# A retention layer and a rational feed-forward on one core: four head units kept whole, values scaled on VectorE, a one-step weight join, and a new order for steps 0 to 31

## The chip, the cores and the metric

One core of a Trainium2 chip runs the whole program. The metric is the device time of one execution in microseconds (us); the time of a kernel is the median of its runs. Engines are called PE (TensorE matmul), PEld (TensorE weight load), DVE (VectorE), ACT (ScalarE), POOL (GpSimd) and SP (SyncE, which issues every DMA here).

## What is computed

```python
scores = scale * q @ k^T                       # 8 batches x 8 heads, 576 positions, 64 wide
ret    = scores * gamma[h] ** (i - j)          # for i >= j, else 0
x      = (ret @ v), heads side by side         # 4608 tokens x 512
h = x @ w_in                                   # 512 -> 2048
P = a0 + a1 h + a2 h^2 + a3 h^3
Q = 1 + |b0| |h| + |b1| h^2
out = (P / (Q + 1e-6)) @ w_out                 # 2048 -> 512
```

All arrays are float32. Dense products are made from two parts of each operand, high and low (tile type fp32r): high by high, high by low and low by high, three matmuls of 128x512 for one.

## The kernel before, in words

**Units.** The 4608 tokens are 36 units of 128 tokens; a batch with its 8 heads is 4.5 units. Unit n has a tile `qk` (q and k transposed, by pairs of heads) and a tile `kv` (k and v with tokens on partitions), each 512 KB, loaded by `load_unit` (lines 104 to 113). The decay is split up: `scale_q` (182) multiplies q by gamma^i on POOL, `scale_v` (187) multiplies v by gamma^-j, eight ACTIVATE instructions of 128x64 with one head's factor each (lines 190 and 191), and what is left of the decay is a mask of zeros and ones. A running state S (64x64 for each head) carries what earlier units give; `fade` (362) multiplies it by gamma^128 on POOL.

**A unit's attention.** A unit is cut in two halves of 64 tokens, so that all its products are 64x64 and four of them can stand in the array. `visit(None, k)` (288) makes the scores of unit k (16 matmuls) and the state's addends (16, less in a batch's first and last half); `decay` (314) multiplies the scores by the mask, `middle` and `add` (331, 351) make the state at the half and at the end; `put` (304) makes the outputs: 24 to 32 matmuls. `emit` (261) interleaves the two rows of the array and sets a SyncE nop between matmuls of different rows that write one bank; SP's later DMAs stand behind these nops. `keep_hi` (342, ACT) and `keep_lo` (345, DVE) take the result out of PSUM as x's two parts.

**Weights.** Each of the 16 blocks of w_in and of w_out comes as 128 x 512 words of 64 bits (512 KB), loaded by `load_weight`. `split_weight` (144) makes two fp32r parts in four stages: ACT scales the high word into `c` with Abs and the low word into `low`; DVE joins them, `c<-c,bits` (line 158); DVE puts the sign back, `c<-bits,c` (line 160); ACT writes the high part `w`, and POOL the difference. The stages are called `split0` to `split3`; `start` begins new blocks.

**Steps.** A step is one block f (128 of the 2048 columns) of one group b of 512 tokens: `gemm1` (12 matmuls into a PSUM tile `h`), `ffn_p`, `ffn_p2`, `ffn_va`, `ffn_v`, `ffn_r`, `ffn_q`, `ffn_q3` for the rational function on ACT and DVE, `ffn_hi` and `ffn_lo` (two parts of `g`), and, three or four steps later, `gemm2` (12 matmuls into `acc`). There are 144 steps: 0 to 7 do half of group 0, 8 to 23 all of group 1, 24 to 31 the other half of group 0, and so on. PSUM tiles `h`, `y` (part of a visit) and the warm-up tile `unread` share two places: a gemm1 can begin when the one two before it has been read, the last reader of `h` being `ffn_p2` on DVE.

**The head.** Before step 0 the program does units 0 to 3 (`before(n)`, line 519, in the order `BEFORE`), with a few idle matmuls `unread` after each (`warm`), then the scores of unit 4 with the outputs of unit 3 (`LAST_BEFORE`). Steps 0, 2, 4 and 6 contain a visit each (outputs of units 4 to 7, scores of 5 to 7).

**What sets the order.** Every engine runs its instructions in program order (`InOrder`, line 59), and the order within a step is written out in lists of names: `FIRST` for steps 0 to 23 with a visit, `FIRST_ALONE` for those without, `MID` for steps 8 to 20, `DENSE` and `DENSE_ALONE` for steps 24 to 31, `REST` and `END` after that (lines 33 to 44; chosen at line 595).

Of the kernel before, what the change touches and what calls it, by code (L numbers as in the profile page):

```python
# [35 lines left out]
FIRST_ALONE = "split1 split3 gemm1 visit gemm2 ffn_p split2 ffn_va ffn_p2 ffn_hi decay keep_hi ffn_lo ffn_r scale_q decay1 add keep_lo fade start scale_v split0 ffn_q ffn_q3 ffn_v".split()
MID = "start split2 gemm1 ffn_p gemm2 ffn_r ffn_hi ffn_lo ffn_va split3 ffn_p2 ffn_q ffn_v ffn_q3 split0 split1".split()
DENSE = "gemm1 ffn_p visit decay split0 ffn_p2 split1 scale_q ffn_hi ffn_r ffn_va ffn_lo scale_v gemm2 ffn_q split2 ffn_v keep_hi split3 ffn_q3 keep_lo decay1 add fade".split()
DENSE_ALONE = "gemm1 ffn_p visit decay keep_hi decay1 add ffn_r split1 fade keep_lo split2 ffn_p2 split0 ffn_va ffn_v scale_q ffn_hi ffn_lo gemm2 split3 scale_v ffn_q ffn_q3".split()
# [598 lines left out]
```

## Time and profile before

| | us |
|---|---|
| median of 3 runs (lowest to highest) | 917.73 (916.36 to 919.26) |
| the profiled execution | 915.75 |
| its span | 913.9 |
| PE busy in the span | 888.9 (97%) |
| DVE busy | 801.1 (88%) |
| ACT busy | 696.2 (76%) |
| POOL busy | 154.3 (17%) |

The profile is one execution, 1.85 us longer than its span of instructions. A row of the timeline reads: start, duration, engine, line, operation, out<-in, count, and in brackets the idle time before it with what ended it. L67 is the line of the helper that records instructions, so work is told by its tiles. A matmul of 64x64 or 128x128 in float32 is two records; one of 128x512 in fp32r is one.

### The profile page before, as it was taken

The page shows a single profiled execution, that of the slowest core. Times are in us where ns is not written, and L with a number is a line of the kernel's source. Part 1 is how long each engine was busy: PE and PEld are TensorE (multiplying, and loading weights), DVE is VectorE, ACT ScalarE, POOL GpSimd, SP SyncE. Part 2 cuts the span into 40 slices and gives each one's busy share as a digit, 9 for nine tenths or more (in the row PEclk, how much of TensorE's full clock was granted, in tenths as well). Part 3 has the DMA queues.
Part 4 walks back from the last instruction along what each step waited for, and adds up shares of the span by engine and source line. Part 5 has one row for each costly group of instructions (what it writes and reads, how often), then busy time and mean ns, then how long its engine had stood idle before and what let it go on. Part 6 is the DMA issues. An engine that isn't in the chain of part 4 may idle for free.

```text
span 913.9 us, 19359 instructions
## 1 busy us (share of the span) xinstructions
PE 888.9 (97%) x7852; PEld 733.1 (80%) x7852; DVE 801.1 (88%) x1217; ACT 696.2 (76%) x1306; POOL 154.3 (17%) x128
## 2 busy tenths in 40 slices
PE   7888999999999999999999999999999999999997
PEld 6666778878888888888888888888888888888886
DVE  3699999998899988889888889889888998888895
ACT  5798899988667778777877787777877777667774
POOL 3556445551011110011100100010110111000000
PEclk8789999999999999999999999999999999999999
DMA  9985000014121112111211112011211121001001
GB/s 340 363 309 202 1 0 1 1 49 138 47 93 48 47 47 93 47 47 47 93 48 48 47 65 74 25 43 33 90 47 48 47 94 47 1 2 46 1 1 46
DMA packets 20569, 65.50 MB, mean 72 GB/s; under 512 B 2432, under 2 KB 2432, under 8 KB 20480
## 3 DMA queue, kind: packets, MB, share of 16 engines
q1 hardware_dynamic: 20480, 64.28, 20.0%
q8 instruction: 61, 1.00, 0.5%
q14 instruction: 28, 0.23, 0.1%
HBM read 54.83 MB, written 9.44 MB: 70 GB/s over the span
## 4 chain that ended last, share of the span: by engine, by line
PE 81%; DVE 13%; issue 2%; ACT 2%; DMA 1%; SPq 0%; ACTq 0%; DVEq 0%
PE acc L67 37%; PE h L67 35%; DVE p L67 6%; PE ps L67 4%; DVE v L67 3%; DVE c L67 3%; PE y L67 2%; PE psNone L67 2%; PE unread L67 1%; DMA gv_sb<-in_gv 1%; ACT free_at L67 1%; DMA bits<-in_w_out 0%; ACT v L67 0%; DVE qk L67 0%; ACT o L67 0%
## 5 line engine op out<-in xcount | busy, mean ns | idle before, releaser
L67 PE MATMUL acc<-w,g 128*128 128x512 f32 x1632 | 396.3, 392 | 0.5 <-DVE o L67 0.3
L67 PE MATMUL h<-xhi,w 128*128 128x512 f32 x1152 | 382.3, 393 | 10.4 <-DVE p L67 6.4
L67 PEld LDWEIGHTS acc<-w,g 128*128 128x128 f32 x1632 | 303.8, 188 | 65.6 <-issue 0.7
L67 PEld LDWEIGHTS h<-xhi,w 128*128 128x128 f32 x1152 | 218.4, 190 | 59.0 <-DVE p L67 8.0
L67 PE MATMUL h<-xlo,w 128*128 128x512 f32 x576 | 226.1, 393 | 0.0
L67 ACT ACTIVATE p<-h,ab_sb 128x512 f32<-128x512 f32 x144 | 111.9, 777 | 127.1 <-PE h L67 117.0
L67 DVE SCALAR_TENSOR_TENSOR p<-p,ab_sb,u 128x512 f32<-128x512 f32 x131 | 120.7, 922 | 15.0 <-ACT u L67 15.0
L67 PEld LDWEIGHTS h<-xlo,w 128*128 128x128 f32 x576 | 109.5, 190 | 22.8
L67 DVE TENSOR_TENSOR p<-p,h 128x512 f32<-128x512 f32 x144 | 98.9, 687 | 29.9 <-ACT u L67 28.9
L67 DVE TENSOR_TENSOR v<-v,u 128x512 f32<-128x512 f32 x131 | 94.7, 723 | 26.5 <-ACT v L67 26.5
L67 ACT ACTIVATE u<-h 128x512 f32<-128x512 f32 x131 | 77.9, 595 | 49.8 <-DVE v L67 49.1
L67 DVE SCALAR_TENSOR_TENSOR p<-p,ab_sb,h 128x512 f32<-128x512 f32 x144 | 107.6, 747 | 4.7
L67 ACT ACTIVATE v<-u,absb 128x512 f32<-128x512 f32 x131 | 105.8, 808 | 1.2 <-DVE p L67 1.1
L67 DVE SCALAR_TENSOR_TENSOR p<-v,p 128x512 f32<-128x512 f32 x144 | 101.3, 703 | 4.4
L67 POOL TENSOR_TENSOR S<-S,gv_sb 128x256 f32<-128x256 f32 x32 | 21.3, 666 | 469.9 <-DVE S L67 446.6
L67 DVE SCALAR_TENSOR_TENSOR v<-v,u 128x512 f32<-128x512 f32 x131 | 95.4, 728 | 0.0
L67 ACT ACTIVATE g<-p 128x512 fp32r<-128x512 f32 x136 | 85.8, 631 | 8.1 <-DVE p L67 3.4
L67 ACT ACTIVATE u<-u 128x512 f32<-128x512 f32 x131 | 83.0, 634 | 4.2
L67 ACT ACTIVATE u<-v 128x512 f32<-128x512 f32 x131 | 81.5, 622 | 0.3 <-DVE v L67 0.3
L67 ACT ACTIVATE kv<-kv,gv_sb 128x64 f32<-128x64 f32 x288 | 72.6, 340 | 8.3 <-DMA gv_sb<-in_gv 5.7
L67 DVE TENSOR_TENSOR g<-p,g 128x512 fp32r<-128x512 f32 x112 | 76.7, 684 | 1.4 <-ACT g L67 1.4
L67 POOL TENSOR_TENSOR qk<-qk,gq_sb 128x512 f32<-128x512 f32 x36 | 56.2, 1562 | 56.7 <-DMA qk<-in_qkv 56.4
(72 smaller groups left out, 715.6 us busy)
## 6 DMA issues: line engine op xcount, KB each, us to landing
qk<-in_qkv SPq DMA_DIRECT2D x36, 512.0 KB, 4.1
kv<-in_qkv SPq DMA_DIRECT2D x36, 512.0 KB, 5.7
bits<-in_w_in SPq DMA_DIRECT2D x16, 512.0 KB, 8.0
bits<-in_w_out SPq DMA_DIRECT2D x16, 512.0 KB, 8.4
out<-o SPq DMA_DIRECT2D x16, 512.0 KB, 4.5
out<-o SPq DMA_DIRECT2D x4, 256.0 KB, 3.6
gq_sb<-in_gq SPq DMA_DIRECT2D x1, 256.0 KB, 2.7
mask_sb<-in_masks SPq DMA_DIRECT2D x1, 32.0 KB, 5.2
```

Source lines behind the costliest of these rows:

```text
L67: return lambda *a, **k: self.tc.keep_in_program_order(method(*a, **k))
```

## The change

1. **Units 0 to 3 whole.** Their attention is no longer cut in halves: scores are 8 matmuls of 128x128, the state's addends 8 over all 128 tokens into a PSUM tile `early` of their own, the outputs 8 with the unit's own scores and 8 with the state: 32 matmuls for up to 64. There is no `emit`, so no SyncE nop. The decay is two DVE instructions of 128x512 with a 128x128 mask, and the state one DVE instruction.
2. **`scale_v` of units 0 to 7** is one DVE multiplication of 128x512; units from 8 on stay on ACT.
3. **Factors in one load.** gq, gv and ab become one array `consts` of 128x530, loaded first; the mask is loaded in two parts, the 128x128 one after unit 0, the old one during unit 1.
4. **Sign by the shift.** ACT's first instruction of a split is Prelu with a slope of -2^32 for negative words in place of Abs; the shift by 3 that joins the words then leaves the sign where it belongs, and `c<-bits,c` is gone: 32 DVE instructions fewer.
5. **Order.** FIRST, FIRST_ALONE, MID, DENSE and DENSE_ALONE are rewritten. In FIRST `ffn_p2` now stands behind the visit's `decay`, `decay1`, `add`; `split3` and `scale_q` are earlier.

```diff
-FIRST = "split1 gemm1 visit ffn_p ffn_p2 ffn_hi split2 decay keep_hi ffn_lo gemm2 ffn_r scale_v scale_q split3 decay1 add fade start split0 keep_lo ffn_q ffn_q3 ffn_va ffn_v".split()
+FIRST = "split1 gemm1 visit ffn_p split3 scale_q ffn_hi split2 decay scale_v keep_hi ffn_lo gemm2 ffn_r decay1 add fade start ffn_va ffn_p2 keep_lo ffn_q ffn_v ffn_q3 split0".split()
...
+FIRST_DENSE_UNIT = 8
...
+    const_sb = const.tile([P, NPAIR * P + H + NPAIR + 6], F32, name="const_sb")
...
-        act.activation(cf, high.bitcast(F32), AF.Abs, scale=math.ldexp(1.0, -112))
+        act.activation(cf, high.bitcast(F32), AF.Prelu, scale=math.ldexp(1.0, -112), alpha=-math.ldexp(1.0, 32))
...
-        dve.scalar_tensor_tensor(c, high, -0x80000000, c, ALU.bitwise_and, ALU.bitwise_or)
...
         v = raws[n][1][:, 1]
+        if n < FIRST_DENSE_UNIT:
+            dve.tensor_tensor(v, v, gv_sb[:, 0:H].unsqueeze(2).broadcast_to([P, H, D]), ALU.mult)
+            return
...
+    early = ps_h.tile([P, 2, NPAIR, D], F32, tag="h", name="early")
+
+    def whole_scores(n):
+        (q, kt), (kn, v) = ([raws[n][w][:, i] for i in range(2)] for w in range(2))
+        ps = sums[n] = place_of(None, n)
+        for g in range(NPAIR):
+            for j in range(2):
+                r = slice(j * D, j * D + D)
+                pe.matmul(ps[:, j, g * P : (g + 1) * P], kt[r, g], q[r, g], start=True, stop=True, skip_group_check=True)
+        for g in range(NPAIR):
+            for j in range(2):
+                pe.matmul(early[j * D : (j + 1) * D, n % 2, g, :], kn[:, 2 * g + j, :], v[:, 2 * g + j, :], start=True, stop=True, skip_group_check=True)
+
+    def whole_decay(n):
+        for j in range(2):
+            m = whole_sb.unsqueeze(1).broadcast_to([P, NPAIR, P])
+            dve.tensor_tensor(whole_ret(n, j), sums[n][:, j].rearrange("p (g i) -> p g i", g=NPAIR), m, ALU.mult)
+
+    def whole_outputs(n):
+        q, v, o = raws[n][0][:, 0], raws[n][1][:, 1], sums_of(n)
+        for j in range(2):
+            ret = whole_ret(n, j)
+            for c in range(2):
+                for e in range(2):
+                    pe.matmul(o[e * D : (e + 1) * D, j, c, :], v[:, 4 * c + 2 * e + j, :], ret[:, 2 * c + e, :], start=c == 0, stop=True, skip_group_check=True)
+        if n % 9:
+            for c in range(2):
+                for j in range(2):
+                    for e in range(2):
+                        r = slice(j * D, j * D + D)
+                        pe.matmul(o[e * D : (e + 1) * D, j, c, :], state[n][r, 2 * c + e, :], q[r, 2 * c + e, :], start=False, stop=True, skip_group_check=True)
+
+    def whole_add(n):
+        S = state[n + 1] = sp.tile([P, NPAIR, D], F32, tag="S", name=f"S{n + 1}")
+        if n % 9 == 0:
+            dve.tensor_copy(S, early[:, n % 2])
+        else:
+            dve.tensor_tensor(S, state[n], early[:, n % 2], ALU.add)
...
-            put(n - 1)
+            if n == 1:
+                nc.sync.dma_start(mask_sb, masks[:, P:])
+            whole_outputs(n - 1)
...
-    nc.sync.dma_start(gq_sb, gq)
+    nc.sync.dma_start(const_sb, consts)
     load_unit(0)
-    nc.sync.dma_start(gv_sb, gv)
-    nc.sync.dma_start(mask_sb, masks)
+    nc.sync.dma_start(whole_sb, masks[:, 0:P])
```

The first place is DVE's row in the head, from the join of weight block 0 of w_in to the last part of x for step 0. A digit in a name is the unit or the block (qk3 is unit 3's tile, psNone_3 its place in PSUM), the last number only a buffer's. Before:

```order
L67 SCALAR_TENSOR_TENSOR c0_0_195<-bits0_0_122,c0_0_195 128x512
L67 SCALAR_TENSOR_TENSOR c0_1_286<-c0_1_286,bits0_1_128 128x512
L67 TENSOR_TENSOR qk3_130<-psNone_3_398,mask_sb_95 128x512
L67 TENSOR_TENSOR kv3_132<-S3_376,psNone_3_398 128x256
L67 TENSOR_TENSOR S4_475<-kv3_132,psNone_3_398 128x256
L67 TENSOR_TENSOR xlo0_282<-psNone_2_298,xhi0_281 128x4x128
L67 SCALAR_TENSOR_TENSOR c0_1_286<-bits0_1_128,c0_1_286 128x512
L67 TENSOR_TENSOR xlo0_282<-psNone_3_398,xhi0_281 128x4x128
```

And the same stretch of the changed kernel:

```order
L68 SCALAR_TENSOR_TENSOR c0_1_216<-c0_1_216,bits0_1_127 128x512
L68 TENSOR_TENSOR kv4_201<-kv4_201,const_sb_95 128x512
L68 TENSOR_TENSOR qk3_129<-psNone_3_279,whole_sb_97 128x512
L68 TENSOR_TENSOR kv3_131<-psNone_3_279,whole_sb_97 128x512
L68 TENSOR_TENSOR S4_323<-S3_265,early_110 128x256
L68 TENSOR_TENSOR xlo0_212<-psNone_2_221,xhi0_211 128x4x128
L68 TENSOR_TENSOR xlo0_212<-psNone_3_279,xhi0_211 128x4x128
```

The two sign instructions are gone; unit 4's values are scaled ahead of unit 3's decay, which is two instructions of 128x512 in place of one and has one state instruction of 128x256 behind it in place of two.

The second place is DVE's row in step 0, with the visit that gives unit 4's outputs and unit 5's scores (y5 and ps4_5); p0_0 and h0_0 belong to step 0. Before:

```order
L67 SCALAR_TENSOR_TENSOR c0_4_554<-c0_4_554,bits0_4_368 128x512
L67 TENSOR_TENSOR p0_0_658<-p0_0_658,h0_0_579 128x512
L67 SCALAR_TENSOR_TENSOR p0_0_658<-p0_0_658,ab_sb_98,h0_0_579 128x512
L67 SCALAR_TENSOR_TENSOR c0_3_548<-bits0_3_273,c0_3_548 128x512
L67 SCALAR_TENSOR_TENSOR c1_0_551<-bits1_0_366,c1_0_551 128x512
L67 SCALAR_TENSOR_TENSOR c0_4_554<-bits0_4_368,c0_4_554 128x512
L67 TENSOR_TENSOR qk5_466<-y5_593,mask_sb_95 128x256
L67 TENSOR_TENSOR kv5_468<-S5_559,y5_593 128x256
```

And now:

```order
L68 COPY S5_389<-psNone_4_352 128x256
L68 TENSOR_TENSOR kv5_316<-kv5_316,const_sb_95 128x512
L68 SCALAR_TENSOR_TENSOR c0_3_378<-c0_3_378,bits0_3_203 128x512
L68 SCALAR_TENSOR_TENSOR c1_0_381<-c1_0_381,bits1_0_256 128x512
L68 SCALAR_TENSOR_TENSOR c0_4_384<-c0_4_384,bits0_4_258 128x512
L68 TENSOR_TENSOR p0_0_480<-p0_0_480,h0_0_401 128x512
L68 TENSOR_TENSOR qk5_314<-y5_415,mask_sb_96 128x256
L68 TENSOR_TENSOR kv5_316<-S5_389,y5_415 128x256
L68 TENSOR_TENSOR qk5_314<-ps4_5_414,mask_sb_96 128x256
L68 TENSOR_TENSOR S6_490<-kv5_316,ps4_5_414 128x256
L68 SCALAR_TENSOR_TENSOR p0_0_480<-p0_0_480,const_sb_95,h0_0_401 128x512
```

The second instruction on p0_0, which is the last reader of h0_0, has moved behind the four instructions of the visit, and the scaling of unit 5's values stands ahead of three joins.

More of the change, by code (lines that the diff above doesn't have):

```diff
@@ L34 @@
 LAST_BEFORE = "visit_b keep_hi visit_a keep_lo start split1 decay add fade scale_q scale_v split2 split3 split0".split()
-FIRST = "split1 gemm1 visit ffn_p ffn_p2 ffn_hi split2 decay keep_hi ffn_lo gemm2 ffn_r scale_v scale_q split3 decay1 add fade start split0 keep_lo ffn_q ffn_q3 ffn_va ffn_v".split()
[L36 to L39, printed above, removed]
+FIRST = "split1 gemm1 visit ffn_p split3 scale_q ffn_hi split2 decay scale_v keep_hi ffn_lo gemm2 ffn_r decay1 add fade start ffn_va ffn_p2 keep_lo ffn_q ffn_v ffn_q3 split0".split()
+FIRST_ALONE = "split1 split3 gemm1 visit scale_v start gemm2 ffn_p ffn_p2 ffn_hi split2 decay keep_hi ffn_r scale_q decay1 add keep_lo fade split0 ffn_q ffn_q3 ffn_lo ffn_va ffn_v".split()
+MID = "start split1 gemm1 ffn_p split2 gemm2 ffn_hi ffn_lo ffn_r ffn_va split0 split3 ffn_p2 ffn_q ffn_v ffn_q3".split()
+DENSE = "gemm1 ffn_p visit decay split0 scale_q ffn_p2 split1 ffn_hi ffn_r ffn_va ffn_lo scale_v gemm2 ffn_q split2 ffn_v split3 keep_hi keep_lo decay1 add ffn_q3 fade".split()
+DENSE_ALONE = "gemm1 ffn_p visit decay keep_hi decay1 add ffn_r split1 fade split0 keep_lo split2 ffn_p2 ffn_va ffn_v scale_q ffn_hi ffn_lo gemm2 split3 scale_v ffn_q ffn_q3".split()
 REST = (
@@ L70, in retention_ffn @@
 @with_exitstack
-def retention_ffn(ctx: ExitStack, tc: tile.TileContext, qkv, w_in, w_out, ab, masks, gq, gv, out):
+def retention_ffn(ctx: ExitStack, tc: tile.TileContext, qkv, w_in, w_out, consts, masks, out):
     nc = tc.nc
@@ L113, in load_unit @@
         raws[n] = qk, kv
+    const_sb = const.tile([P, NPAIR * P + H + NPAIR + 6], F32, name="const_sb")
+    gq_sb = const_sb[:, 0 : NPAIR * P].rearrange("p (g i) -> p g i", g=NPAIR)
+    gv_sb = const_sb[:, NPAIR * P : NPAIR * P + H + NPAIR]
+    ab_sb = const_sb[:, NPAIR * P + H + NPAIR :]
     mask_sb = const.tile([P, D], F32, name="mask_sb")
-    gv_sb = const.tile([P, H + NPAIR], F32, name="gv_sb")
-    gq_sb = const.tile([P, NPAIR, P], F32, name="gq_sb")
-    ab_sb = const.tile([P, 6], F32, name="ab_sb")
+    whole_sb = op.tile([P, 2, DM], F32, tag="o0", name="whole_sb")[:, 0, 0:P]
     absb = const.tile([P, 2], F32, name="absb")
@@ L194, in halves, with place_of @@
         return x.rearrange("p (g d) -> p g d", d=D)
+    def place_of(a, k):
+        by_acc = k is not None and k <= NP and k != 2
+        pool_, tag = (ps_acc, "acc") if by_acc else (ps_at, "at")
+        return pool_.tile([P, 2, 512], F32, tag=tag, name=f"ps{a}_{k}")
     def places(a, k):
         apart = a is None or k is not None and k <= NP
-        by_acc = apart and k <= NP and k != 2
-        pool_, tag = (ps_acc, "acc") if by_acc else (ps_at, "at")
-        ps = pool_.tile([P, 2, 512], F32, tag=tag, name=f"ps{a}_{k}")
+        ps = place_of(a, k)
         if a is not None and not apart:
@@ L259, in of_before, with whole_ret @@
         return made
+    early = ps_h.tile([P, 2, NPAIR, D], F32, tag="h", name="early")
[9 more added lines that the diff above has]
+                pe.matmul(early[j * D : (j + 1) * D, n % 2, g, :], kn[:, 2 * g + j, :], v[:, 2 * g + j, :], start=True, stop=True, skip_group_check=True)
+    def whole_ret(n, j):
+        return raws[n][0][:, 1] if j == 0 else raws[n][1][:, 0].rearrange("p (g x) d -> p g (x d)", g=NPAIR)
+    def whole_decay(n):
[21 more added lines that the diff above has]
+            dve.tensor_tensor(S, state[n], early[:, n % 2], ALU.add)
     def emit(*rows_of):
@@ L520, in start_scores @@
         def start_scores():
-            visit(None, n)
+            if n < NP:
+                whole_scores(n)
+            else:
+                visit(None, n)
             if n + 1 < len(WARM):
@@ L536, in before @@
         todo |= {f.__name__: (f, n + 1) for f in (scale_q, scale_v)}
+        if n < NP:
+            todo |= {"decay": (whole_decay, n), "add": (whole_add, n)}
         if n >= 1:
@@ L602, in _tables @@
     scale = 1.0 / np.sqrt(D)
-    masks = np.tile(t[None, :D] >= t[:D, None], (2, 1))
+    upper = t[None, :] >= t[:, None]
+    masks = np.concatenate([upper, np.tile(upper[:D, :D], (2, 1))], axis=1)
     rows = np.repeat(gamma.reshape(NPAIR, 2), D, axis=1).T
@@ L608, in _tables @@
     gv = np.concatenate([gamma[None, :] ** -t[:, None], rows**P], axis=1)
-    return [np.ascontiguousarray(x, dtype=np.float32) for x in (masks, gq, gv)]
+    return [np.ascontiguousarray(x, dtype=np.float32) for x in (masks, gq.reshape(P, NPAIR * P), gv)]
 def kernel(q, k, v, moe_w_in, moe_w_out, moe_a, moe_b):
@@ L622 @@
         "w_out": np.ascontiguousarray(moe_w_out).view(np.int64).reshape(NF, P, DM),
-        "ab": np.ascontiguousarray(np.broadcast_to(np.concatenate([moe_a, moe_b]), (P, 6))),
+        "consts": np.concatenate([gq, gv, np.broadcast_to(np.concatenate([moe_a, moe_b]), (P, 6))], axis=1),
         "masks": masks,
-        "gq": gq,
-        "gv": gv,
     }
```

2 lines of the change are left out of this document (removed).

## The prediction

> **What bounds the kernel now.** I first cut the span into stages with the windows view: up to the first gemm1, steps 0 to 7, the next seven steps, and the rest. Columns: stage and length, then busy us (instructions) of each engine, the clock granted to PE, DMA.
>
> ```profile
> 0.00:33.10 33.10, 25.98 (x589) 23.05 (x589) 11.73 (x21) 18.57 (x55) 11.53 (x15) 0.74 0.95 360
> 33.10:94.50 61.40, 50.95 (x592) 39.82 (x590) 59.49 (x85) 53.49 (x107) 33.78 (x24) 0.89 0.72 258
> 94.50:132.60 38.10, 36.26 (x158) 29.05 (x157) 34.85 (x51) 35.90 (x63) 17.60 (x13) 1.00 0.00 1
> 132.60:200.00 67.40, 66.86 (x455) 54.91 (x454) 66.66 (x100) 63.24 (x120) 34.36 (x27) 1.00 0.05 17
> 200.00:800.00 600.00, 599.71 (x5531) 496.47 (x5530) 537.02 (x825) 449.16 (x848) 57.01 (x51) 1.00 0.17 57
> ```
>
> From 200 us on PE has no idle time (599.71 of 600), and nothing there is changed. What the change can win lies before: PE idle 7.1 us in the first stage, 10.5 in the second, 1.8 in the third, 0.5 in the fourth, and work at a clock below 1 in the first two. In the second stage DVE is the full engine: 59.49 of 61.40. The view of waits says the same of the whole run, and PE's timeline shows where (start, duration, what, and in brackets idle time and its releaser):
>
> ```profile
> PEld h L67 <- DVE p L67: 8.0, 5, 2.8
> PE h L67 <- DVE p L67: 6.4, 3, 2.7
> ```
>
> ```profile
> 33.09 0.50 PE L67 MATMUL h<-xhi,w 128*128 128x512 f32 x1
> ...
> 41.21 0.50 PE L67 MATMUL h<-xhi,w 128*128 128x512 f32 x1 [2.12 <-DVE p L67]
> ...
> 55.16 0.79 PE L67 MATMUL h<-xhi,w 128*128 128x512 f32 x1 [2.66 <-DVE p L67]
> ...
> 86.94 0.74 PE L67 MATMUL h<-xhi,w 128*128 128x512 f32 x1 [3.07 <-ACT w L67]
> ...
> 94.48 0.39 PE L67 MATMUL h<-xhi,w 128*128 128x512 f32 x1
> ```
>
> So steps 0, 1, 3, 7 and 8 start there; three of them late, twice because DVE had not read an older h, once because a weight block came late out of its split. A matmul behind an idle gap also takes longer (0.79 against 0.39 us), so a gap costs more than its length.
>
> **The head: step 0 starts earlier.** Units arrive one after another, and before step 0 the chain of unit 3 ends last:
>
> ```profile
> 11.26 2.02 ACT L67 ACTIVATE kv<-kv,gv_sb 128x64 f32<-128x64 f32 x8 [1.52 <-DMA kv<-in_qkv]
> 15.03 2.02 ACT L67 ACTIVATE kv<-kv,gv_sb 128x64 f32<-128x64 f32 x8 [0.61 <-DMA kv<-in_qkv]
> 19.19 2.02 ACT L67 ACTIVATE kv<-kv,gv_sb 128x64 f32<-128x64 f32 x8 [0.50 <-DMA kv<-in_qkv]
> 23.27 1.01 PE L67 MATMUL psNone<-qk 64*64 64x64 f32 x25 [2.43 <-issue]
> 25.28 0.69 DVE L67 TENSOR_TENSOR qk<-psNone,mask_sb 128x512 f32<-128x512 f32 x1 [1.66 <-PE psNone L67]
> 29.59 0.71 PE L67 MATMUL psNone<-qk,kv 64*64 64x64 f32 x16
> 31.76 0.94 PE L67 MATMUL psNone<-qk 64*64 64x64 f32 x32
> 32.05 0.60 ACT L67 ACTIVATE xhi<-psNone 128x512 fp32r<-128x512 f32 x1 [2.02 <-PE psNone L67]
> 32.68 0.69 DVE L67 TENSOR_TENSOR xlo<-psNone,xhi 128x512 fp32r<-128x512 f32 x1 [3.37 <-ACT xhi L67]
> ```
>
> Unit 3's values are there at 19.19, but its scores end only at 25.28 (2.43 us of that PE waited for nothing that the profile shows, among many small matmuls), its outputs begin at 29.59 behind unit 2's, and x is complete at 33.37. In the changed kernel the values need one DVE instruction (0.69 us, as the xlo row of the same shape) for 2.02 us on ACT, and unit 2's outputs can run before unit 3's decay. But in DVE's row the scaling of kv4 now stands ahead of unit 3's decay, and so decay, state and x wait for kv4's landing. The landings are 3.77 and 4.16 us apart; at the last distance kv4 lands at 23.35. From there: scaling 0.7 to 1.7 (below), two decays from 0.6 apart to the end of the second, 1.3, unit 3's outputs 2.0 (the 64x64 form: 1.47 us below, 2.17 from 29.59 to 31.76), xhi 0.6, xlo 0.7: 23.35 + 1.2 + 1.3 + 2.0 + 0.6 + 0.7 = 29.1. The scores of unit 4, about 1.3 us (31.76 to 33.09), run beside xhi and xlo. So step 0 starts at 29.0 and not 33.09: **-4.1 us**, between -2.5 (scaling 1.7, outputs 2.4, a slow clock on the scores) and -5.5 (0.7 and 1.5).
>
> What the whole products cost PE is not in the trace. Bounds:
>
> ```profile
> 14.90 1.47 PE L67 MATMUL psNone<-qk,kv 64*64 64x64 f32 x48
> ...
> 16.30 0.94 PE L67 MATMUL unread<-gq_sb 128*128 128x128 f32 x6
> ...
> 17.16 0.77 PE L67 MATMUL psNone<-qk 64*64 64x64 f32 x31
> ```
>
> One 128-column record after another takes (0.94 - 0.22)/5 = 0.144 us; 64-column records in four places of the array come every (0.77 - 0.22)/30 = 0.018 us, a quarter of half that. 128-column records in two places should come every 0.072 us, so a unit needs 16 x 0.072 (scores) + 16 x 0.036 (addends) + 16 x 0.072 + 16 x 0.036 (outputs) = 3.5 us, against 2.3 us for 128 records at 0.018. Half the products is thus no less PE time, only fewer instructions; it stays under the 4.16 us between landings, and the cover is the load. Without any overlap it would be 48 x 0.144 + 16 x 0.072 = 8.1 us (a rival).
>
> One load of factors saves 0.2 us at most, since landings set the pace. The nops that go free SP, whose loads of the head run at full rate already (DMA share 0.95): counted at nothing.
>
> **Steps 0 to 7: DVE's load.** The groups of DVE and ACT in the second stage (count | busy, mean ns | idle before):
>
> ```profile
> L67 DVE SCALAR_TENSOR_TENSOR c<-bits,c 128x512 int32<-128x512 int32 x13 | 10.7, 846 | 0.0
> L67 DVE SCALAR_TENSOR_TENSOR c<-c,bits 128x512 int32<-128x512 int32 x13 | 10.5, 829 | 0.0
> ```
>
> ```profile
> L67 ACT ACTIVATE v<-u,absb 128x512 f32<-128x512 f32 x8 | 6.5, 814 | 0.6 <-DVE p L67 0.5
> L67 ACT ACTIVATE c<-bits 128x512 f32<-128x512 f32 x12 | 8.0, 666 | 0.0
> L67 ACT ACTIVATE kv<-kv,gv_sb 128x64 f32<-128x64 f32 x24 | 6.0, 344 | 0.0
> ```
>
> ```profile
> 33.28 0.68 DVE L67 SCALAR_TENSOR_TENSOR c<-c,bits 128x512 int32<-128x512 int32 x1
> 33.88 0.68 DVE L67 TENSOR_TENSOR qk<-psNone,mask_sb 128x512 f32<-128x512 f32 x1
> ```
>
> Instructions follow each other 0.60 apart though each lasts 0.68, so 0.08 of each is overlap. Gone: 13 sign instructions, 10.7 - 13 x 0.08 = 9.7 us. New: values of units 5, 6 and 7, 3 x 0.61 = 1.8. DVE's work falls by 7.8 us, and DVE has next to no other idle time to give back: **-7.8 us**. The cover is gone from two sides. A scaling can meet a POOL instruction:
>
> ```profile
> 18.02 1.28 POOL L67 TENSOR_TENSOR qk<-qk,gq_sb 128x512 f32<-128x512 f32 x1 [1.90 <-DMA qk<-in_qkv]
> 18.17 1.68 DVE L67 SCALAR_TENSOR_TENSOR c<-c,bits 128x512 int32<-128x512 int32 x1
> ```
>
> Here a DVE instruction with two SBUF operands took 1.68 us for 0.68 while POOL ran, and `scale_q` of the same unit is just such a POOL instruction, which on ACT did no harm. The Trainium skill (SBUF — State Buffer, section "SBUF: two separate sides") says why: the port pair is "an exclusive lock, not a bandwidth split", and whoever comes second blocks for the whole instruction; ScalarE has its own port. The trace agrees with it (1.0 us late behind a POOL instruction of 1.28). If every one of the three meets POOL it is 3 x 1.0 us, and kv5's landing (six transfers of 512 KB after kv4 at 4.16/3 = 1.4 us or less, about 31) holds DVE another 0.5: -4.3 us. On the other side, in step 0 `ffn_p2` now waits for the visit's four instructions, but three sign instructions that stood after it are gone too, so step 1 starts by my count about 4 us before 41.21, with nothing lost of the head's gain. What is late next is PE itself: its 50.95 us at a clock of 0.89 are 45.3 at full clock, so the stage can't go under that; 61.4 - 7.8 = 53.6 leaves DVE still the limit.
>
> ACT loses 6.0 us of `kv` and keeps its 12 Prelu at 0.67, as Abs; what Prelu costs is not in the trace, and the nearest row is Abs; the dearest form of 128x512 on ACT there takes 0.81, and 12 x 0.15 more would be 1.8 us, less than the 6.0 that went. ACT still has one table load in its whole row, so Prelu brings none.
>
> **Steps 8 to 14 and after.** In the third stage PE idles 38.10 - 36.26 = 1.84 us. DVE loses 7 sign instructions there, but ACT has 35.90 of 38.10 and loses nothing (values of the visited units only lie before): of the 1.84, **-1.3 us**, between -0.5 and -1.84. From 132.6 to 200 PE idles 0.54 us; new orders there are counted at nothing, -0.5 to +0.5.
>
> **Sum.** -4.1 - 7.8 - 1.3 = -13.2 us, ends -7.3 (2.5 + 4.3 + 0.5) and -19.8 (5.5 + 12 + 1.8 + 0.5, where 12 is halfway from 7.8 to the 16.1 at which only PE's own 45.3 are left). The profiled execution took 915.75 us, a span of 913.9 and 1.85 around it: 902.5 after. It lies 2.0 under the median of 917.73, so the forecast for a median is 904.5.
>
> **The rivals.**
> - *The head gives little (0.07).* Landings and POOL hold DVE more often than I count, and the gain is 2.8 to 7.3 us: about 912.5. For it: the second stage's DMA share of 0.72 and three scalings that wait for landings at the head of DVE's row. Against it: the 13 sign instructions go whatever the landings.
> - *PE alone remains (0.06).* The new order hides DVE entirely: stage two 45.3 for 61.4, -16.1, with -4.1 and -1.8 a total of -22: 895.7. Against it: 59.49 - 7.8 = 51.7 us of DVE work are more than 45.3.
> - *No change (0.04).* DVE's sign work was slack, and the waits pass to ACT (53.49 of 61.40) at the same place: 917.7 within 2.75 us, the 0.3% that a measurement of this kernel can tell. Against it: ACT too loses 6.0 us.
> - *Slower: whole products one after another (0.05).* If pairs of 64x128 and 128x64 do not run side by side, PE needs 8.1 us a unit, over the 4.16 between landings, from 8.2 on (unit 0's values 3.77 before unit 1's, and 0.7 to scale them): four units and three warm-ups of 0.94 end at 43.4, x is complete 1.3 later, step 0 starts 11.6 late. Less 7.8 and 1.3 that is +2.5: 920. It decides from 7.5 us a unit on. For it: no such product is in the trace; its four 64x64 forms do overlap. The Trainium skill (TensorEngine Tiling (Array Packing), section "Key Properties") says that changing the tiling mode "drains the TensorE", which this change does about five times a unit for two. In the row at 17.16 the 64x64 form starts before the 128x128 one of 16.30 ends (17.24), so the trace shows no price; at 0.22 us, one record's length, 20 drains are 4.4 us, mostly under loads.
>
> Forecast 0.78. Faster by over 0.3%: 0.78 + 0.07 + 0.06 = 0.91; within: 0.04; slower: 0.05. The forecast's own ends are 897.9 and 910.4; with part of the first rival, 898 to 911.
>
> **What would show it.** Right: step 0's first gemm1 at 28 to 30.5; step 8's at 81 to 84 (94.48 less 11.9); no `c<-bits,c`; DVE still at 90% or more between them; PE's idle time from step 8 to 15 under 1 us; from step 32 on everything shifted by one constant. Wrong: step 0 after 32, unit products over 4.2 us, a Prelu of 1 us or more, scaled values on DVE at 1.7 us each, or PE idle in steps 8 to 31 that before did not have.

## The result and the profile after

The changed kernel takes 902.0 us (median; 901.43 to 902.4) beside 917.43 for the kernel before: 0.983 of its time, with a 95% interval of 0.981 to 0.985. Its profiled execution took 901.43 us, a span of 899.7, 14.2 less than before. Two executions of the last experiment below, at a mean granted clock of 0.56 and 0.65, took 1475.84 and 1260.83 us and are left out of its median. The windows view, cut at the same steps of the program as in the prediction:

```profile
0.00:27.80 27.80, 22.60 (x332) 19.75 (x332) 14.15 (x24) 8.39 (x14) 12.68 (x15) 0.94 0.94 363
27.80:82.90 55.10, 46.62 (x592) 36.90 (x589) 54.68 (x73) 46.94 (x83) 34.19 (x24) 0.97 0.87 320
82.90:119.20 36.30, 35.77 (x158) 29.25 (x158) 30.99 (x46) 35.50 (x62) 17.30 (x13) 1.00 0.01 3
119.20:185.60 66.40, 66.40 (x455) 54.86 (x454) 59.88 (x89) 63.35 (x120) 34.27 (x26) 1.00 0.06 17
185.60:785.60 600.00, 599.72 (x5530) 496.42 (x5529) 536.98 (x825) 448.88 (x846) 58.28 (x51) 1.00 0.17 57
```

In the second line DVE is still full (54.68 of 55.10), with 12 instructions fewer; ACT lost 6.5 us of work. The third and fourth line hold next to no idle time of PE (0.53 and 0.00), and the fifth is what it was. PE's timeline gives the starts of steps 0, 1, 3, 7 and 8:

```profile
27.83 0.49 PE L68 MATMUL h<-xhi,w 128*128 128x512 f32 x1
...
36.44 0.47 PE L68 MATMUL h<-xhi,w 128*128 128x512 f32 x1 [2.19 <-DVE kv L68]
...
48.93 0.76 PE L68 MATMUL h<-xhi,w 128*128 128x512 f32 x1 [3.10 <-DVE kv L68]
...
77.10 0.39 PE L68 MATMUL h<-xhi,w 128*128 128x512 f32 x1
...
82.95 0.39 PE L68 MATMUL h<-xhi,w 128*128 128x512 f32 x1
```

The late weight block ahead of step 7 is no more. Steps 1 and 3 still start late, but the releaser has another name: not `p` (the last read of h) but `kv`, which is the visit's read of its tile y. The chain of work that ended last, by engines, first before and then after, says the same in one line each:

```profile
PE 81%; DVE 13%; issue 2%; ACT 2%; DMA 1%; SPq 0%; ACTq 0%; DVEq 0%
```

```profile
PE 88%; DVE 5%; ACT 4%; DMA 1%; issue 1%; SPq 0%; DVEq 0%; ACTq 0%
```

DVE's share of that chain fell from 13% to 5%. What went, by stage, from the starts of steps 0, 8, 15 and 32 (us; step 15 at 132.57 before and 119.16 after, step 32 at 238.81 and 224.44):

| | before | after | change | term of the prediction |
|---|---|---|---|---|
| to step 0 | 33.09 | 27.83 | -5.26 | -4.1 |
| steps 0 to 7 | 61.39 | 55.12 | -6.27 | -7.8 |
| steps 8 to 14 | 38.09 | 36.21 | -1.88 | -1.3 |
| steps 15 to 31 | 106.24 | 105.28 | -0.96 | 0 |

After step 32 everything is 14.4 us earlier, by one constant.

### The profile page after: what moved, and what is told of

It is laid out like the page before. It is cut to its first block, busy times and chain, and to the rows that moved or that the text cites. A ratio compares the mean times of both kernels' runs of the same rounds, so it can differ in the third digit from the quotient of the medians.

```text
span 899.7 us, 18728 instructions
## 1 busy us (share of the span) xinstructions
PE 880.3 (98%) x7596; PEld 727.0 (81%) x7596; DVE 788.1 (88%) x1193; ACT 678.9 (75%) x1242; POOL 156.7 (17%) x128
## 4 chain that ended last, share of the span: by engine, by line
PE 88%; DVE 5%; ACT 4%; DMA 1%; issue 1%; SPq 0%; DVEq 0%; ACTq 0%
PE acc L68 42%; PE h L68 39%; PE ps L68 4%; PE y L68 2%; DVE p L68 2%; DMA kv<-in_qkv 1%; DVE c L68 1%; DVE v L68 1%; PE psNone L68 1%; ACT bits L68 1%; DVE kv L68 1%; DVE qk L68 0%; ACT free_at L68 0%; ACT c L68 0%; ACT u L68 0%
## 5 line engine op out<-in xcount | busy, mean ns | idle before, releaser
L68 ACT ACTIVATE p<-h,const_sb 128x512 f32<-128x512 f32 x144 | 111.7, 776 | 127.3 <-PE h L68 122.0
L68 DVE SCALAR_TENSOR_TENSOR p<-p,const_sb,u 128x512 f32<-128x512 f32 x131 | 117.8, 900 | 15.6 <-ACT u L68 15.5
L68 DVE TENSOR_TENSOR v<-v,u 128x512 f32<-128x512 f32 x131 | 96.7, 738 | 25.7 <-ACT v L68 25.7
L68 DVE SCALAR_TENSOR_TENSOR p<-p,const_sb,h 128x512 f32<-128x512 f32 x144 | 107.6, 747 | 4.8
L68 DVE SCALAR_TENSOR_TENSOR p<-v,p 128x512 f32<-128x512 f32 x144 | 104.2, 724 | 4.3
L68 POOL TENSOR_TENSOR S<-S,const_sb 128x256 f32<-128x256 f32 x32 | 21.9, 684 | 474.6 <-DVE S L68 431.6
L68 DVE SCALAR_TENSOR_TENSOR v<-v,u 128x512 f32<-128x512 f32 x131 | 93.1, 711 | 0.0
L68 POOL TENSOR_TENSOR qk<-qk,const_sb 128x512 f32<-128x512 f32 x36 | 57.3, 1593 | 53.2 <-DMA qk<-in_qkv 51.6
L68 ACT ACTIVATE kv<-kv,const_sb 128x64 f32<-128x64 f32 x224 | 56.4, 340 | 0.0
```

Of the source, the lines that this page charges most:

```text
L68: return lambda *a, **k: self.tc.keep_in_program_order(method(*a, **k))
```

## The experiments

Each experiment starts from the changed kernel unless it says otherwise, and its ratio is to the kernel before, run beside it on the same chip. 0.983 [0.981, 0.985] is the changed kernel's.

### The sign instruction put back

```diff
-        act.activation(cf, high.bitcast(F32), AF.Prelu, scale=math.ldexp(1.0, -112), alpha=-math.ldexp(1.0, 32))
+        act.activation(cf, high.bitcast(F32), AF.Abs, scale=math.ldexp(1.0, -112))
...
+        dve.scalar_tensor_tensor(c, high, -0x80000000, c, ALU.bitwise_and, ALU.bitwise_or)
```

> The changed kernel with the sign instruction back: Abs on ScalarE, and the 32 VectorE instructions c<-bits,c. Theory (VectorE's work sets steps 0 to 7): 13 of them lie there, 9.7 us by their rows, 7 more in the third stage with 1.5 us, so 911 us (908 to 913), step 0 unmoved at 27.8 and step 8 at 90 to 92 for 82.95. Rival (the order and the whole units give most, sign work fits into slack): at most 905, step 8 before 86.

919.1 us, 1.002 [1.001, 1.003]: the whole gain is gone, 17.1 us, far more than either theory gave it; without the shift the other four parts together make the kernel no faster than it was. Its windows, cut at steps 0, 8 and 15, the last with as many PE records as the fourth line above:

```profile
27.70:90.70 63.00, 50.86 (x588) 40.56 (x589) 62.46 (x85) 48.11 (x83) 35.22 (x25) 0.86 0.76 280
90.70:131.30 40.60, 37.05 (x157) 28.72 (x156) 38.66 (x54) 37.09 (x62) 17.43 (x13) 1.00 0.01 2
131.30:202.20 70.90, 69.35 (x456) 54.87 (x456) 70.13 (x99) 64.64 (x118) 34.04 (x26) 1.00 0.05 16
```

Step 0 is as early as in the changed kernel (27.70), and steps 0 to 7 take 63.0 for 55.1, as the theory said. What it left out is the rest: in the second and third line DVE is full as well (38.66 of 40.60, 70.13 of 70.90), and PE idles 3.55 and 1.55 us where the changed kernel has 0.53 and none. The three stages are 7.9, 4.3 and 4.5 us longer, so more than half of the loss lies behind step 8.

### The shift alone, in the kernel before

```diff
-        act.activation(cf, high.bitcast(F32), AF.Abs, scale=math.ldexp(1.0, -112))
+        act.activation(cf, high.bitcast(F32), AF.Prelu, scale=math.ldexp(1.0, -112), alpha=-math.ldexp(1.0, 32))
...
-        dve.scalar_tensor_tensor(c, high, -0x80000000, c, ALU.bitwise_and, ALU.bitwise_or)
```

> The kernel before with one part of the change alone: Prelu and no sign instruction, old order, units cut, values on ScalarE. Theory (VectorE's sign work set the pace of steps 0 to 7): step 0 unmoved at 33, step 8 some 7 us earlier than 94.48, the third stage 1.8 us shorter: 908.5 us (907 to 911). Rival (without the other parts the waits pass to the cut units, POOL or ScalarE): 913 or more.

909.41 us, 0.992 [0.990, 0.993]: 7.6 us, within the theory's range. The windows of steps 0 to 7, 8 to 14 and 15 to 31:

```profile
33.10:91.80 58.70, 51.53 (x591) 40.89 (x590) 53.19 (x72) 52.42 (x107) 33.27 (x24) 0.90 0.74 268
91.80:127.40 35.60, 35.60 (x158) 29.24 (x157) 29.69 (x44) 35.25 (x62) 16.68 (x13) 1.00 0.00 0
...
127.40:233.00 105.60, 105.60 (x965) 87.28 (x964) 95.03 (x146) 94.22 (x187) 42.80 (x35) 1.00 0.16 51
```

But the time lies elsewhere than expected. DVE's work in steps 0 to 7 falls by 6.3 us (59.49 to 53.19), and the stage shortens by 2.7 only: in the old order DVE now stands idle 5.5 us there. Steps 8 to 14 give 2.5 and steps 15 to 31 another 0.6, so that PE has no idle time left in either; with a head that ends at 33.09 as before, these account for 5.8 of the 7.6, and the rest lies within what one profiled execution differs from a median. So the shift has two prices: 7.6 us by itself, and 17.1 once the order has been built on it.

### The five lists of the order as before

FIRST, FIRST_ALONE, MID, DENSE and DENSE_ALONE are those of the kernel before; all else is changed.

```diff
-FIRST = "split1 gemm1 visit ffn_p split3 scale_q ffn_hi split2 decay scale_v keep_hi ffn_lo gemm2 ffn_r decay1 add fade start ffn_va ffn_p2 keep_lo ffn_q ffn_v ffn_q3 split0".split()
+FIRST = "split1 gemm1 visit ffn_p ffn_p2 ffn_hi split2 decay keep_hi ffn_lo gemm2 ffn_r scale_v scale_q split3 decay1 add fade start split0 keep_lo ffn_q ffn_q3 ffn_va ffn_v".split()
```

> The changed kernel with the five order lists of before. Theory: VectorE's work is the same, so steps 0 to 7 lose only what its instructions wait for at its head; step 1 again waits for ffn_p2 and step 7 for its weight block: 904.5 us (903 to 907). Rival (the new order is the larger half of the gain): 908 or more.

905.83 us, 0.988 [0.986, 0.989]: the order is worth 3.8 us, as expected. Its window of steps 0 to 7:

```profile
30.10:88.70 58.60, 50.48 (x592) 39.90 (x589) 55.65 (x75) 47.91 (x83) 33.34 (x24) 0.88 0.77 288
```

Steps 0 to 7 take 58.6 us, the same as with the shift alone, for 55.1 with the new lists: PE again waits for `p` ahead of steps 1 and 3 (2.22 and 3.06 us) and for a weight block ahead of step 7 (1.15). Step 0 was 2.3 us later in this execution because kv4 came at 23.98 and its scaling met POOL (1.75 us); the new lists have no part in that.

### Units 0 to 3 cut in halves as before

```diff
-            if n < NP:
-                whole_scores(n)
-            else:
-                visit(None, n)
+            visit(None, n)
...
-            whole_outputs(n - 1)
+            put(n - 1)
...
-        if n < NP:
-            todo |= {"decay": (whole_decay, n), "add": (whole_add, n)}
```

> The changed kernel with units 0 to 3 cut in halves as before (64x64 products, SyncE nops, the old mask loaded first). Theory: whole units cost PE as much time (3.5 us a unit) and save only instructions; step 0 starts 1 to 3 us later than 27.8, and since step 0's visit waits for unit 5's landing most of that is hidden: 903.5 us (902.5 to 905). Rival (half the products are the head's gain): 906 to 907.5, step 0 at 32 or later and everything behind it as late.

With the products the old decay, the SyncE nops and the old mask's place in the loads come back. 906.08 us, 0.988 [0.986, 0.990]: whole units are worth 4.1 us, the rival's number and not the theory's. Step 0 starts at 32.50, 4.7 us later than in the changed kernel. The granted clock is not the reason, being 0.95 up to step 0 here and 0.94 in the changed kernel. PE's timeline has rows that wait for no semaphore that the profile shows:

```profile
17.80 0.50 PE L68 MATMUL psNone<-qk 64*64 64x64 f32 x18 [0.57 <-issue]
...
23.91 0.92 PE L68 MATMUL psNone<-qk 64*64 64x64 f32 x25 [2.70 <-issue]
...
29.93 0.27 PE L68 MATMUL unread<-const_sb 128*128 128x128 f32 x1 [1.44 <-issue]
```

The kernel before has such stops too, 2.43 us at 23.27 (shown in the prediction) and 0.60 at 29.29, and so has the run of the shift alone (0.43, 2.57 and 2.87); the changed kernel has none over 0.4 us ahead of step 0. Counted by PE's matmul records from the start, the three stops stand behind records 221, 348 and 475, which are 127 apart.

### The same, with six warm-up matmuls fewer ahead

To see whether the stops belong to the tiles or to the place in PE's stream, 12 records of the warm-up at the start, ahead of unit 0, were taken out of the kernel of the last experiment:

```diff
-WARM = [8, 3, 2]
+WARM = [2, 3, 2]
```

> Units 0 to 3 cut as in the run before on cut units, with two idle matmuls at the start in place of eight: 12 matmul records fewer ahead of everything. There PE stood still 2.70 and 1.44 us with nothing to wait for, 127 matmul records apart: behind the 6th record of unit 3's scores and behind the 5th of the third warm-up. Theory (the stops belong to places in PE's instruction stream): they come 12 records later, behind the 18th record of unit 3's scores and 127 records after it, among unit 3's outputs. Rival (they belong to a time or to a tile): at the old tiles.

```profile
16.87 0.34 PE L68 MATMUL psNone<-qk 64*64 64x64 f32 x7 [1.07 <-issue]
...
22.98 0.59 PE L68 MATMUL psNone<-qk 64*64 64x64 f32 x11 [2.67 <-issue]
...
29.00 0.28 PE L68 MATMUL psNone<-qk,kv 64*64 64x64 f32 x3 [1.37 <-issue]
```

It took 904.67 us in its one execution. The stops are behind records 221, 348 and 475 again, and so each stands 12 records further on in the program: behind the 25th record of unit 2's scores for the 13th, further into unit 3's scores, in unit 3's outputs for a warm-up. They belong to the place in PE's stream of instructions, 127 matmuls apart.

What PE lacks there is in the view of DMA queues. Besides the loads it has a queue of another kind, here in the run with the units cut:

```profile
q8 instruction: 61, 1.00, 0.5%
```

These are 61 transfers of 16384 bytes for 7852 matmul records (59 for 7596 in the changed kernel), one for each 127 or so. In the four traces with cut units there are 11 such stops, of 0.43 to 2.87 us, and each ends 1.25 to 1.61 us after one of these transfers has landed: here the transfers landed at 16.43, 22.48 and 28.62 us. So PE waits, by all that the traces show, for its own instructions, which arrive among loads at a DMA share of 0.95, and between two stops it gets through 127 records no faster than in 6.0 us. Whole units have 332 records in the head for 588, and 127 of them take 7.8 and 9.2 us; the transfers for records 222 and 349 land 5.1 and 5.4 us before PE needs them, and no stop is seen. In the run with the units cut the stops sum to 4.71 us, and its step 0 is 4.67 us late; that all of it comes from them is argued from these sums.

### The values on ACT again

```diff
-FIRST_DENSE_UNIT = 8
+FIRST_DENSE_UNIT = 0
```

> The changed kernel with the values of all units scaled on ScalarE, as before. Theory: in steps 0 to 7 three VectorE instructions go (0.69, 1.78 and 0.68 us in the changed kernel's trace), and in the head unit 3's decay no longer waits behind unit 4's values: 899.5 us (898 to 901.5), faster than the changed kernel's 902.0. Rival (ScalarE had to be relieved; its 44.7 busy us of 52.9 in steps 0 to 7 become the limit with 6 more): 904 to 908.

901.83 us, 0.983 [0.982, 0.985]: the same as the changed kernel; both theories missed, from opposite sides. The window of steps 0 to 7, and the wait on DVE behind unit 6's values on ACT (39.81 to 41.7):

```profile
28.50:83.70 55.20, 48.28 (x592) 38.83 (x589) 50.40 (x71) 52.51 (x107) 31.96 (x24) 0.91 0.84 317
```

```profile
44.12 0.69 DVE L68 TENSOR_TENSOR p<-p,h 128x512 f32<-128x512 f32 x1 [2.41 <-ACT u L68]
```

DVE loses 4.3 us of work, ACT gains 5.6, and the stage takes 55.2 as before. Moving the values to DVE is worth nothing by itself: in this order the one engine waits for the other to the same end. The clock leaves a doubt: it was 0.91 in this window for 0.97 in the changed kernel's, and PE was busy 1.7 us longer (48.28 for 46.62), which may have hidden a small gain.

### No subtraction on POOL

The low parts of all weights are left out: POOL writes zeros in their place, so that the two inputs that it read are not read.

```diff
-        pool.tensor_tensor(w[:, 1, :], cf, w[:, 0, :].bitcast(F32), ALU.subtract)
+        pool.memset(w[:, 1, :].bitcast(F32), 0.0)
```

> The changed kernel with POOL's subtraction, which makes the low parts of the weights from two SBUF operands, replaced by a POOL memset of zeros: low parts of all weights are left out of the result. Theory (what is left in steps 0 to 7 is VectorE stretched by POOL, instructions of 0.68 us that take 1.76 beside POOL): some eight of them go back to 0.7, step 8 comes at 76 to 79 for 82.95, total 896 to 898.5. Rival (steps 0 to 7 are set by landings, ScalarE or PE, and the stretch is slack): 900.5 to 902.5.

898.54 us, 0.980 [0.978, 0.981], at the upper end of the theory's range and out of the rival's; step 8 came at 79.83, later than the 76 to 79 expected. Its window of steps 0 to 7, and then the joins of that window:

```profile
28.20:79.80 51.60, 46.16 (x592) 37.26 (x589) 46.04 (x75) 47.26 (x84) 20.44 (x24) 0.97 0.89 338
```

```profile
L68 DVE SCALAR_TENSOR_TENSOR c<-c,bits 128x512 int32<-128x512 int32 x13 | 10.0, 797 | 0.0
```

With two instructions more than in the changed kernel DVE is busy 8.6 us less (46.04 for 54.68): the scaled values take 0.69 us each for 1.05, the joins 0.80 for 1.17. These 8.6 us are what POOL's subtraction, set against a memset, costs DVE in steps 0 to 7, and 3.5 us of them reach the stage. POOL's own row also became shorter (20.44 for 34.19), and the run doesn't separate the two.

### The visit ahead of the splits in FIRST

Step 1 waits for DVE's read of y, which stands behind joins of splits. Here `split1` and `split2` stand at the end of the list; nothing else moves.

```diff
-FIRST = "split1 gemm1 visit ffn_p split3 scale_q ffn_hi split2 decay scale_v keep_hi ffn_lo gemm2 ffn_r decay1 add fade start ffn_va ffn_p2 keep_lo ffn_q ffn_v ffn_q3 split0".split()
+FIRST = "gemm1 visit ffn_p split3 scale_q ffn_hi decay scale_v keep_hi ffn_lo gemm2 ffn_r decay1 add fade start ffn_va ffn_p2 keep_lo split1 split2 ffn_q ffn_v ffn_q3 split0".split()
```

> The changed kernel with split1 and split2 behind the visit in FIRST: in steps 0, 2, 4 and 6 the joins of weight blocks no longer stand ahead of p and of the visit's decay on VectorE; the instructions are the same. Theory A (the amount of VectorE's work in steps 0 to 7 is the limit): step 1 starts up to 1.6 us earlier, but steps 3 to 8 give it back, 901.5 us (901 to 902.4). Theory B (the order at the head of VectorE's row is, since PE waits for the visit's read of y): 900 or less, step 1 at 34.8 and step 8 at 81.5 or earlier.

902.21 us, 0.985 [0.983, 0.986]: no difference from the changed kernel, as theory A has it. PE's starts of steps 1, 3 and 8, and the window:

```profile
34.82 0.47 PE L68 MATMUL h<-xhi,w 128*128 128x512 f32 x1 [0.70 <-DVE kv L68]
...
49.08 0.77 PE L68 MATMUL h<-xhi,w 128*128 128x512 f32 x1 [1.49 <-ACT u L68]
...
83.28 0.39 PE L68 MATMUL h<-xhi,w 128*128 128x512 f32 x1
```

```profile
28.10:83.30 55.20, 48.45 (x594) 38.80 (x590) 52.60 (x72) 47.07 (x83) 32.18 (x24) 0.91 0.85 314
```

Step 1 is 1.6 us earlier, and step 3 is where it was: its wait has passed to ACT, and step 8 starts as late as ever. The wait for `kv` was a place where the stage's lack showed, not its cause. Here too the clock was 0.91 in the window, and PE was busy 1.8 us longer than in the changed kernel (48.45 for 46.62); what the order would give at the same clock is open.

### The scaling of q first in FIRST_ALONE

```diff
-FIRST_ALONE = "split1 split3 gemm1 visit scale_v start gemm2 ffn_p ffn_p2 ffn_hi split2 decay keep_hi ffn_r scale_q decay1 add keep_lo fade split0 ffn_q ffn_q3 ffn_lo ffn_va ffn_v".split()
+FIRST_ALONE = "split1 scale_q split3 gemm1 visit scale_v start gemm2 ffn_p ffn_p2 ffn_hi split2 decay keep_hi ffn_r decay1 add keep_lo fade split0 ffn_q ffn_q3 ffn_lo ffn_va ffn_v".split()
```

> The changed kernel with scale_q at the front of FIRST_ALONE, so that POOL scales the next unit's q before three weights' low parts; the visits of steps 2 and 4 waited 1.42 and 0.36 us for it. Theory (VectorE is the limit there): PE waits less at y6 and as much more at the next gemm1, 901.5 us (900.8 to 902.4). Rival (the wait is on the path): 900.4 or less.

902.72 us, 0.984 [0.982, 0.985]: no difference, 0.3 above the theory's range. In steps 0 to 7 PE's waits for POOL's scaled q fell from 2.5 to 0.9 us, but step 3 waits 3.10 us for `kv` as before:

```profile
51.43 0.76 PE L68 MATMUL h<-xhi,w 128*128 128x512 f32 x1 [3.10 <-DVE kv L68]
```

### The decay of unit 3 ahead of unit 4's values, and both orders together

```diff
-BEFORE = "split1 start scale_q scale_v visit_a decay visit_b add fade keep_hi keep_lo split2 split3 split0".split()
+BEFORE = "split1 start scale_q visit_a decay visit_b add scale_v fade keep_hi keep_lo split2 split3 split0".split()
```

> The changed kernel with scale_v behind decay and add in the head's order, so that unit 3's decay does not wait for unit 4's values to land. Theory: decay of unit 3 starts when its scores are done, about 1.4 us earlier counted from the landing of unit 4, and step 0 about 1 us; step 1 then waits for unit 5's landing as before: 901.5 us (900.8 to 902.2). Rival (the head's gain goes through to the end): 900.4 to 901.

900.98 us, 0.983 [0.981, 0.984]. PE's starts of steps 0 and 8:

```profile
26.15 0.50 PE L68 MATMUL h<-xhi,w 128*128 128x512 f32 x1
...
81.75 0.39 PE L68 MATMUL h<-xhi,w 128*128 128x512 f32 x1
```

In its profiled execution step 0 is 1.7 us earlier and step 8 is 1.2 earlier, but the medians are 1.0 apart and the intervals overlap: whether it is faster stays open, and 900.98 lies in the ranges of both the theory and the rival. Together with the visit ahead of the splits in FIRST:

> The same FIRST together with scale_v behind decay and add in the head. Theory A: 900.5 us (899.8 to 901.3), as the head's order alone (901.0). Theory B: 898 to 899.5.

901.1 us, 0.984 [0.982, 0.985], within theory A's range. Theory B's further gain is out. No version that does all of the work beats the changed kernel by more than its interval.

## Why the prediction was right

The total was right: -13.2 forecast, -14.2 in the span of the profiled executions, -15.4 between the medians. The four terms of the table are off by 1.2, 1.5, 0.6 and 1.0 us, the second against the other three, so that the total is nearer than its terms deserve. By its steps:

**The head, -4.1 by the sum, -5.26 measured.** The rows from kv4's landing to step 0, DVE's row first, then ACT's, then PE's:

```profile
22.57 1.44 DVE L68 TENSOR_TENSOR kv<-kv,const_sb 128x512 f32<-128x512 f32 x1 [0.23 <-DMA kv<-in_qkv]
23.94 0.68 DVE L68 TENSOR_TENSOR qk<-psNone,whole_sb 128x512 f32<-128x512 f32 x1
24.54 0.68 DVE L68 TENSOR_TENSOR kv<-psNone,whole_sb 128x512 f32<-128x512 f32 x1
...
27.66 0.69 DVE L68 TENSOR_TENSOR xlo<-psNone,xhi 128x512 fp32r<-128x512 f32 x1 [1.52 <-ACT xhi L68]
```

```profile
27.03 0.60 ACT L68 ACTIVATE xhi<-psNone 128x512 fp32r<-128x512 f32 x1 [2.54 <-PE psNone L68]
```

```profile
15.79 1.16 PE L68 MATMUL psNone<-qk 64*128 64x128 f32 x16
16.88 0.69 PE L68 MATMUL early<-kv 128*64 128x64 f32 x16
17.40 0.61 PE L68 MATMUL psNone<-qk,kv 128*64 128x128 f32 x8
17.84 0.61 PE L68 MATMUL psNone<-kv 128*64 128x128 f32 x8
18.38 0.67 PE L68 MATMUL psNone<-qk,S 64*64 64x128 f32 x16
...
25.27 0.66 PE L68 MATMUL psNone<-qk,kv 128*64 128x128 f32 x8 [1.09 <-DVE kv L68]
```

Up to the outputs the chain is the one that the prediction wrote down: landing, scaling, two decays, outputs. kv4 landed at 22.55, not 23.35, which is 0.8 of the 1.2 us too much won. The scaling took 1.44 for 1.2 and met POOL as feared, though a weight's subtraction (21.75 to 23.47) and not the scaling of q; the outputs took 1.70 for 2.0. Step 0 began 0.86 us behind them and not 1.3: its first matmul needs xhi but not xlo, which ended at 28.35 with step 0 under way, and what came last was PE's own scores of unit 4. The landing is partly luck, since kv4 came between 22.55 and 24.07 in the runs with whole units; it came at 24.07 in the profiled execution of the run with `scale_q` first, which took 903.37 us. One load of factors alone was not tried.

The credit went to the wrong part. The prediction gave the head's gain to the values on DVE and the earlier decay. But with the units cut again, and both of these kept, step 0 came at 32.50, so that 0.6 of the 5.26 us are left; and with the values on ACT it came at 28.50, though unit 4's values landed 1.06 us later than in the changed kernel. Nearly all of the gain is that of the whole units.

**Whole products, 3.5 us a unit.** They took 1.16 for the scores, 0.69 for the addends and 1.64 for the outputs (17.40 to 19.04); the rows overlap, and from start to start it is 3.2 us (15.79 to the warm-up at 18.97). So the estimate was a little high, and the rival of products one after another is out. The change of form seems to have a price, which the prediction read as none: in the trace's single records of unit 2 the first record of a new form starts 0.20 us after the last of the old one, at all four changes, where inside the rows the next pair of records mostly follows after 0.05 to 0.11. By an estimate from these spacings that is 0.4 us a unit. What the prediction did not see is why fewer instructions help. It named PE's 2.43 us as idle time without a cause; cutting the units again brings 4.1 us back, with stops on PE of 0.57, 2.70 and 1.44 us, each of them ended by an instruction transfer.

**Steps 0 to 7, -7.8 by the sum, -6.27 measured: the mis-sized term.** DVE's busy time fell by 4.8 us and not by 7.8; the other 1.5 us of the stage are DVE's own idle time (1.91 us before, 0.42 after), of which the prediction held there was next to none to give. The groups of that stage after, and four of them before:

```profile
L68 DVE SCALAR_TENSOR_TENSOR c<-c,bits 128x512 int32<-128x512 int32 x12 | 13.7, 1171 | 0.0
L68 DVE TENSOR_TENSOR v<-v,u 128x512 f32<-128x512 f32 x7 | 6.6, 945 | 0.1
L68 DVE SCALAR_TENSOR_TENSOR p<-v,p 128x512 f32<-128x512 f32 x6 | 6.3, 1057 | 0.1
L68 DVE SCALAR_TENSOR_TENSOR v<-v,u 128x512 f32<-128x512 f32 x6 | 5.6, 935 | 0.0
L68 DVE SCALAR_TENSOR_TENSOR p<-p,const_sb,u 128x512 f32<-128x512 f32 x6 | 5.0, 841 | 0.0
L68 DVE TENSOR_TENSOR kv<-kv,const_sb 128x512 f32<-128x512 f32 x3 | 3.1, 1049 | 0.1
```

```profile
L67 DVE SCALAR_TENSOR_TENSOR v<-v,u 128x512 f32<-128x512 f32 x6 | 6.7, 1115 | 0.0
L67 DVE SCALAR_TENSOR_TENSOR p<-p,ab_sb,u 128x512 f32<-128x512 f32 x6 | 6.3, 1042 | 0.0
L67 DVE TENSOR_TENSOR v<-v,u 128x512 f32<-128x512 f32 x7 | 5.7, 811 | 0.7 <-ACT v L67 0.7
L67 DVE SCALAR_TENSOR_TENSOR p<-v,p 128x512 f32<-128x512 f32 x6 | 5.4, 904 | 0.2
```

The prediction took the sign instructions at their mean of 0.846 us. A sign instruction that meets no POOL work lasts 0.68 and stands 0.60 from the next; the other part of its mean was POOL's stretch, and POOL's work did not go (33.78 us before, 34.19 after). So the stretch fell on other instructions: the joins went from 829 to 1171 ns, the seven `v<-v,u` from 811 to 945, `p<-v,p` from 904 to 1057, while the six `v<-v,u` and `p<-p,u` became shorter (1115 to 935, 1042 to 841); taken together, the five groups gained 3.7 us. Counted at 0.60 each the sum would have been 13 x 0.60 - 3 x 0.61 = 6.0. The two runs on the sign alone bear this out: 13 instructions carry 6.3 us of DVE's work in the old order (59.49 to 53.19) and 12 carry 7.8 in the new (62.46 to 54.68), 0.48 and 0.65 us each, for 0.75 in the sum. The three values, in turn, took 3.1 us for 1.8. The run without POOL's subtraction shows the other side of it: joins of 797 ns, values of 687. The Trainium skill (SBUF — State Buffer, section "SBUF: two separate sides"), which the prediction used for the values alone, calls the shared port pair an exclusive lock; these rows agree. By it the price hangs on POOL's instructions and not on which DVE instruction with two SBUF inputs meets them.

Where the gain lies is telling too. Of the 6.27 us, 4.9 lie between the starts of steps 6 and 8 (76.60 to 94.48 before, 69.98 to 82.95 after), where PE no longer waits for the weight block; the six steps ahead give only 1.4.

**Step 1's start.** The prediction had it wait for `ffn_p2` behind the visit, 4 us before 41.21. It started at 36.44, 4.8 earlier, though counted from step 0 it is 0.5 later than before (8.61 for 8.12), and for another reason: it waited for the visit's read of y (DVE `kv`, 35.89 to 36.29), and `ffn_p2` ran after that, at 36.88. The place in PSUM that gemm1 needed was y's and not h0_0's, which was still unread: here it is not the tile two before that counts. The visit ahead of the splits moved that wait by 1.6 us and the end of the stage by nothing.

**Steps 8 to 14 and 15 to 31, -1.3 and 0 by the sum, -1.88 and -0.96 measured.** PE's idle time fell by just the 1.3 us forecast in the first (1.84 to 0.53), and by 0.54 in the fourth line of the windows, which the prediction counted at nothing, within 0.5. The rest is in PE's busy time, with nearly the same records: 36.26 to 35.77, and 66.86 to 66.40. A matmul behind a gap takes longer, and the prediction's terms counted the gaps at their length. But its 0.79 and 0.74 us for steps 3 and 7 are mostly the clock: those rows, and the 0.76 of step 3 above, lie in stretches where the granted clock was 0.50 (52.9 to 59.7 and 87.0 to 90.4 us before, 48.4 to 51.8 after). At a clock of 1.00, which these two stages have, it is 0.47 to 0.50 for 0.39 (36.44 here, 41.21 before). The shift alone takes PE's idle time out of both stages, so that a few us of DVE work were on the path there.

**Prelu** took 663 ns (19 of them in steps 0 to 14) beside 666 for Abs, no dearer.

**What each part is worth**, taken alone or undone: the shift 7.6 us in the kernel before, 17.1 undone in the changed one; whole units 4.1, the order 3.8, the values on DVE 0. The four do not add up: the new order is built on the shorter split, and without the shift all other parts together leave 919.1 us. Steps 0 to 7 have no single limit left: less DVE work with more ACT work changes nothing, less stretch by POOL gives 3.5 us. Which of ACT's and DVE's chains decides each step there was not settled. Of the prediction's signs, step 8 (82.95), DVE's share, PE's idle time from step 8 to 15 (0.53) and the constant shift came as said; step 0 came 0.2 us ahead of its stretch, and one value of three on DVE took 1.78 us, which it had named as a sign of being wrong.

## What to carry to other kernels

When an instruction goes from an engine that another engine stretches, count it at its undisturbed spacing: the stretch belongs to the disturber and lands on other instructions that meet it. Undo a part both in the old and in the new kernel before giving it a price; here the same edit was worth 7.6 us in the one and 17.1 in the other. Many small matmuls under full loads can outrun the arrival of PE's own instructions; here 332 records in the head for 588 took the stops away. And a wait that ends late is a cause only if the end of its stage moves when the wait goes.

## What was not expected of the hardware

While loads fill the DMA engines (share 0.95), PE with cut units stops 127 matmul records apart, with as many weight loads between, for 0.43 to 2.87 us, until 1.25 to 1.61 us after a 16384-byte transfer of kind "instruction" has landed; 12 records taken away shift the stops by 12 in the program. And loads land differently from one execution to the next, which here carried through to the end of the run. DVE's first scaling of values in the changed kernel, and then in the run with `scale_q` first:

```profile
7.54 0.69 DVE L68 TENSOR_TENSOR kv<-kv,const_sb 128x512 f32<-128x512 f32 x1 [6.54 <-DMA kv<-in_qkv]
```

```profile
9.65 0.69 DVE L68 TENSOR_TENSOR kv<-kv,const_sb 128x512 f32<-128x512 f32 x1 [8.65 <-DMA kv<-in_qkv]
```

Unit 0's values came 2.1 us later, with the same loads in the same order ahead of them as in the changed kernel, whose execution was 1.9 us shorter.
